# Query and key casts behind the preceding pair's first row maxima, one transfer per operand, one task per pair for PV, in a fused attention and MoE kernel on one Trainium2 core

## The chip, the cores and the metric

One core of a Trainium2 chip runs the whole program. The metric is the device time in microseconds (us), median of the runs shown.

## The reference

Three stages follow each other, all in float32. Attention has 4 batches, 8 heads, 576 rows and 64 columns per head; a routed mixture of 8 experts (top 1, 512 to 1024 to 512) and a three-way maximum layer (512 to 768 to 512) follow on the 2304 tokens.

```python
scores = scale * np.matmul(q, k.transpose(0, 1, 3, 2))
cum = np.cumsum(np.log(np.clip(f, 0.0001, 1.0)), axis=-1)
scores = np.where(causal, -1e9, scores + cum[:, :, :, None] - cum[:, :, None, :])
attn = np.exp(scores - scores.max(-1, keepdims=True))
attn = attn / (attn.sum(-1, keepdims=True) + 1e-09)
x = np.matmul(attn, v)                       # B, H, S, D -> B*S, H*D
...
expert_idx = np.argmax(logits, axis=1)       # logits = normed x @ normed emb.T / tau
out[mask] = gate_w[mask, None] * (np.maximum(x[mask] @ w1[e], 0.0) @ w2[e])
...
h = np.maximum(np.maximum(x @ w1, x @ w2), x @ w3)
return h @ w_out
```

## The kernel before, in words

Attention works on 16 pairs of heads (p = 0 to 15, four pairs to a batch). A float32 product is made of rounded high parts and remainders: for each pair, `At` holds q rounded in its rows 0 to 63 and the remainder of q in rows 64 to 127, `R1` holds k rounded (both halves), `R2` the remainder of k in rows 0 to 63 and the decay (`chi`, `clo`) in rows 64 and 65, and `Bt` a copy of rounded q with two rows of ones. A score tile is one matmul of At with R1 and one of Bt with R2 (L355 for block 0 of both heads, L360 for the others). The work that makes these operands, per pair, is in `split_tasks` (L313): loads of q and k by SP (`load_pair`), the two rounding casts `q_hi` and `k_hi` on ACT or DVE (L462 on DVE, L464 on ACT), the two remainders `k_lo` (L334) and `q_lo` (L331) on POOL, and the copy to Bt by a DMA (`q_copy`). Each operand exists three times, so pair p writes over that of pair p - 3. For pair 0 it is written out ahead of the plan (`first_split`, L274 to 281).

Blocks of rows are taken in the order 4, 0, 3, 1, 2. For each, DVE subtracts the mask and takes the row maxima (L383, L377 for block 0), ACT takes the exponential (L408), PE transposes (L421 to L429), and DVE or ACT copies into `PT` (L462, L464). `pair_out` then makes reciprocals (L473 to L476), the product with V in two groups of columns (`pv`, L488, tiles po_0 and po_1), copies them (`ot`), transposes them back with the expert embedding appended (`back`, L507, tiles pb_0 and pb_1), normalises (`norm`, L516) and stores. After the last pair of a batch a routing chain follows on DVE (L604 to L618 and further operations).

What stands on which engine, and in which order, is decided while the program is built, by a planner (`Sched`, L128): each task has an engine (or two to choose from), a cost, a priority and the tasks that it depends on; the planner takes the task that can start first, and of those that can start together the one of lowest priority number. A task with `get` needs a buffer of a pool: three score tiles `s`, eight probability tiles `P`, two `t`, two `o`, two `ot`. The order on each engine is then fixed; on the chip every instruction waits for its operands. The setup of the routing constants, among it `tri8` (L579), runs as a chain in the same plan.

```python
load = sd.task("SP", 3.3, lambda e: load_pair(p), u - 8, ready[p - 2], lat=2.0)
qh = sd.task(("ACT", "DVE"), (1.02, 0.67), q_hi, u, old + [load])
kh = sd.task(("ACT", "DVE"), (1.1, 0.8), k_hi, u, old + [load, qh])
kl = sd.task("Pool", 2.6, k_lo, u, [kh])
ql = sd.task("Pool", 2.6, q_lo, u, [qh, kl])
```

Of the kernel before, what the change touches and what calls it, by code (L numbers as in the profile page):

```python
# [6 lines left out]
F32 = mybir.dt.float32  # L7
# [122 lines left out]
class Sched:  # L130
# [8 lines left out]
        self.bias = {"DVE": 0.15, "Pool": 2.0}  # L139

    def task(self, eng, cost, fn, prio, deps=(), get=None, rel=(), lat=0.0):
        t = Task(eng if isinstance(eng, tuple) else (eng,), cost, fn, prio, get, rel, lat)
        t.deps = [d for d in deps if d is not None]
        for d in t.deps:
            if d.end is None:
                d.after.append(t)
                t.wait += 1
        if not t.wait:
            self.open.append(t)
        return t  # L150
# [27 lines left out]
    def when(self, t, eng):  # L178
        r = self.clk.get(eng, self.t0)
        for d in t.deps:  # L180
            r = max(r, d.end + (self.HOP if d.by != eng else 0.0))
        if t.get:
            pool, _ = t.get
            held = self.taken[pool]
            n = len(held) - self.bufs[pool]
            if n >= 0:
                if (pool, held[n]) not in self.freed:
                    return None
                r = max(r, self.freed[pool, held[n]] + self.HOP)
        return r  # L190

    def run(self):
        while self.open:
            best = None
            for t in self.open:
                pick = None
                for i, eng in enumerate(t.eng):
                    r = self.when(t, eng)
                    if r is None:
                        break  # L200
                    c = t.cost[i] if isinstance(t.cost, tuple) else t.cost
                    k = r + c + self.bias.get(eng, 0.0)
                    if pick is None or k < pick[0]:
                        pick = k, r, eng, c
                if pick and (best is None or (pick[1], t.prio) < best[0]):
                    best = (pick[1], t.prio), t, pick[2], pick[3]
            (r, _), t, eng, c = best
            self.open.remove(t)
            self.clk[eng] = r + c
            self.now, self.later = t, []  # L210
            t.by = eng
            t.end = r + c + t.lat
            if t.get:
                self.taken[t.get[0]].append(t.get[1])
            t.fn(eng)
            for k in t.rel:
                self.freed[k] = r + c
            for add, spec, deps in self.later:
                add(spec, deps)
            self.done(t, r + c + t.lat, eng)  # L220


def attention(tc, g, qT, kT, v, x_dram, es):
# [30 lines left out]
    def load_pair(p):  # L254
        q2 = ld.tile([128, 2, S], F32, tag="q2", name=f"q2_{p}")
        k2 = ld.tile([128, 2, S], F32, tag="k2", name=f"k2_{p}")
        for t, src in ((q2, qT), (k2, kT)):
            for r in range(2):
                nc.sync.dma_start(out=t[64 * r:64 * r + 64], in_=src[p])
        raws[p] = q2, k2  # L260

    def load_v(b):
# [51 lines left out]
    def split_tasks(p):  # L314
        i, u = p % NQ, 10 * p - 6
        load = None
        if p > 1:
            old = [fs[h, t, k] for h in (2 * p - 6, 2 * p - 5) for t in range(NBLK) for k in range(1 + (t == 4))] if p >= NQ else []
            load = sd.task("SP", 3.3, lambda e: load_pair(p), u - 8, ready[p - 2], lat=2.0)
            dec = sd.task("SP", 1.3, lambda e: load_decay(p), u - 4, old, lat=2.0)  # L320
        else:
            old, dec = [], None

        def q_hi(e):
            evict(e, At[i], raws[p][0])

        def k_hi(e):
            evict(e, R1[i], raws[p][1])

        def q_lo(e):  # L330
            nc.gpsimd.tensor_tensor(out=At[i][64:128], in0=raws[p][0][64:128], in1=At[i][64:128].bitcast(F32), op=ALU.subtract)  # L331

        def k_lo(e):
            nc.gpsimd.tensor_tensor(out=R2[i][0:64], in0=raws[p][1][0:64], in1=R1[i][0:64].bitcast(F32), op=ALU.subtract)  # L334

        def q_copy(e):
            nc.sync.dma_start(out=Bt[i][0:64].bitcast(F32), in_=At[i][0:64].bitcast(F32))

        qh = sd.task(("ACT", "DVE"), (1.02, 0.67), q_hi, u, old + [load])
        qc = sd.task("SP", 0.9, q_copy, u, [qh], lat=2.0)  # L340
        kh = sd.task(("ACT", "DVE"), (1.1, 0.8), k_hi, u, old + [load, qh])
        kl = sd.task("Pool", 2.6, k_lo, u, [kh])
        ql = sd.task("Pool", 2.6, q_lo, u, [qh, kl])
        ready[p] = [x for x in (qh, ql, qc, kh, kl, dec) if x is not None]
# [45 lines left out]
    def head(h):  # L390
# [3 lines left out]
        for t in order:  # L394
# [14 lines left out]
                                     accum_out=sums[b][0:n, t, h % H:h % H + 1])  # L409

            fe[h, t] = sd.task("ACT", 0.28 + ext / 1200, exp, slot[h, t], [fr[h, t]])
        old = [fo[p - 2, u] for u in range(2)] if p >= 2 else []
        low = [slice(64 * x, 64 * x + 64) for x in range(2)]
        for t in order:
            i0 = ROW0[t]
# [44 lines left out]
    def evict(e, out, in_):  # L460
        if e == "DVE":
            nc.vector.tensor_copy(out, in_)  # L462
        else:
            nc.scalar.activation(out=out, in_=in_, func=AF.Copy)  # L464

    def pair_out(p):
# [9 lines left out]
            nc.vector.reciprocal(rs[0], rs[0])  # L476

        rt = sd.task("DVE", 0.35, recip, u0, [fe[h, t] for h in hs for t in order])
        for u, (c0, w) in enumerate(RNG):
            na = 3 if u == 0 else 5  # L480
            o = {}

            def pv(e, u=u, c0=c0, w=w, na=na, o=o):
                po = o[0] = ps_o.tile([128, 512], F32, tag="o", name=f"po_{p}_{u}")
                for a in range(na):
                    lo = max(128 * a, c0)
                    for r in range(2):
                        nc.tensor.matmul(po[64 * r:64 * r + 64, lo - c0:w],  # L488
                                         vt[b][:, a, (2 * hp + r) * D:(2 * hp + r + 1) * D],
                                         PT[(2 * p + r) % NPT][:, a, lo:c0 + w], start=(a == 0), stop=(a == na - 1))  # L490

            ts = order
            cost = sum((c0 + w - max(128 * a, c0)) * 4 / 2400 + 0.05 for a in range(na))
            fo[p, u] = sd.task("PE", cost, pv, u0 + 1, [fv[h, t] for h in hs for t in ts] + [vdep[b]], get=("o", ("po", p, u)))

            def cp_(e, u=u, w=w, o=o):
                o[1] = op.tile([128, 320], F32, tag="ot", name=f"ot_{p}_{u}")
                evict(e, o[1][:, 0:w], o[0][:, 0:w])

            fc = sd.task(("ACT", "DVE"), (act(w), dve(w)), cp_, u0 + 2 * u - 4, [fo[p, u]], get=("ot", (p, u)), rel=[("o", ("po", p, u))])  # L500
            m = len(BLKS[u])

            def back(e, u=u, c0=c0, m=m, o=o):
                pb = o[2] = ps_o.tile([128, 512], F32, tag="o", name=f"pb_{p}_{u}")
                for j, t in enumerate(BLKS[u]):
                    i0 = ROW0[t] - c0
                    nc.tensor.matmul(pb[:, 144 * j:144 * j + 144], o[1][:, i0:i0 + 128],  # L507
                                     g.w144[:, hp].rearrange("p r c -> p (r c)"), start=True, stop=True)

            fb = sd.task("PE", 0.24 * m, back, u0 + 2 * u + 1, [fc, consts_done], get=("o", ("pb", p, u)), rel=[("ot", (p, u))])  # L510

            def norm(e, u=u, m=m, o=o):
                if hp == 0 and u == 0:
                    XL[b] = xl.tile([128, NBLK, H, DW], F32, tag="XL", name=f"XL{b}")
                t0 = BLKS[u][0]
                nc.vector.tensor_tensor(  # L516
                    out=XL[b][:, t0:t0 + m, 2 * hp:2 * hp + 2, :], in0=o[2][:, 0:144 * m].rearrange("p (s r c) -> p s r c", s=m, r=2),
                    in1=rs[0][:, t0:t0 + m].unsqueeze(3).to_broadcast([128, m, 2, DW]), op=ALU.mult)

            fn_[p, u] = sd.task("DVE", 0.07 + 0.15 * m, norm, u0 + 2 * u - 4, [fb, rt], rel=[("o", ("pb", p, u))])  # L520
# [17 lines left out]
    split_tasks(1)  # L538
    for p in range(NP):
        b, hp = divmod(p, NPAIR)  # L540
        if p + 2 < NP:
            split_tasks(p + 2) if p + 2 > 1 else None
        if hp == 1 and b + 1 < B:
            vdep[b + 1] = sd.task("SP", 3.3, lambda e, b=b: load_v(b + 1), 40 * b + 20, [fo[NPAIR * b - 1, u] for u in range(2)] if b else [], lat=2.0)
        head(2 * p)
        head(2 * p + 1)
        pair_out(p)
        if hp == NPAIR - 1:
            batch_out(b)
# [940 lines left out]
```

## Time and profile before

| what | before |
|---|---|
| time, median of 3 runs | 766.96 us (765.95 to 769.46) |
| the profiled execution | 767.35 us, span of the trace 765.5 us |
| mean granted clock of TensorE | 0.98 of full speed |
| PE busy, in matmul | 723.9 us, 95% of the span |
| DVE, ACT, POOL busy | 59%, 49%, 18% |
| q and k in DRAM | 32 transfers each of 288 KB, 64 partitions |
| PE's last matmul of attention ends at about | 210 us |

The profiled execution is one run; its span leaves out 1.85 us around the trace. PE is the engine that is busy nearly all the time; the other engines matter where PE waits for them. Granted clock is the share of TensorE's full clock that was granted over a stretch.

### The profile page before, as it was taken

The numbers are of one execution on the slowest core, as the hardware profiler recorded it, in microseconds if no ns is written. First come the engines' busy times: TensorE is split into PE (matmuls) and PEld (weight loads), VectorE is DVE, ScalarE is ACT, GpSimd is POOL, SyncE is SP. The second block draws the span as 40 slices with busy tenths as digits, with TensorE's granted clock in tenths as the row PEclk, the third lists the DMA queues.
The fourth block names the chain that finished last, engine by engine and source line by source line (L and its number), as shares of the span: only waits on it lengthen the run. The fifth ranks groups of instructions, "written<-read, shape, count | busy, mean of one in ns | idle before, by whom it ended". The sixth has DMA issues, their size and how long they took to land. (4 is left out here: it accounts for less than half of the span.)

```text
span 765.5 us, 13139 instructions
## 1 busy us (share of the span) xinstructions
PE 723.9 (95%) x4814; PEld 679.8 (89%) x4814; DVE 449.1 (59%) x1101; ACT 376.8 (49%) x871; POOL 138.9 (18%) x124
## 2 busy tenths in 40 slices
PE   1899999899949999999999999999999999999996
PEld 1688888788839999999999999989999899998994
DVE  6878888787576986888787759722212123122220
ACT  5588899699637655555565645421211212112111
POOL 7555373532030201202101000010010100101001
PEclk9999999899959999999999999999999999999999
DMA  9778886751155656647566443110000100100001
GB/s 224 201 171 188 220 199 177 167 126 33 33 176 193 223 196 203 203 148 250 190 212 244 169 166 91 49 42 0 15 29 1 42 1 0 42 1 28 15 0 44
DMA packets 44612, 90.17 MB, mean 118 GB/s; under 512 B 23320, under 2 KB 23320, under 8 KB 44544
## 3 DMA queue, kind: packets, MB, share of 16 engines
q1 hardware_dynamic: 40416, 77.70, 35.3%
q0 software_dynamic: 3152, 9.88, 3.6%
q10 hardware_dynamic: 976, 1.70, 0.6%
q8 instruction: 40, 0.66, 0.4%
q14 instruction: 28, 0.23, 0.1%
HBM read 74.97 MB, written 9.44 MB: 110 GB/s over the span
## 5 line engine op out<-in xcount | busy, mean ns | idle before, releaser
L1267 DVE TENSOR_TENSOR tm<-pm,tm 128x384 f32<-128x384 f32 x72 | 40.1, 557 | 178.8 <-PE pm L937 178.6
L937 PE MATMUL pm<-x_y,m 128*128 128x384 f32 x432 | 144.4, 334 | 0.0
L935 PE MATMUL pm<-x_y,m 128*128 128x384 f32 x432 | 144.4, 334 | 0.0
L936 PE MATMUL pm<-x_y,m 128*128 128x384 f32 x432 | 144.4, 334 | 0.0
L981 DVE TENSOR_TENSOR w<-stg,w 128x1024 fp32r<-128x1024 f32 x64 | 77.9, 1223 | 26.1 <-ACT w L964 25.8
L408 ACT ACTIVATE P<-P,nm 128x576 f32<-128x576 f32 (+2 forms) x144 | 84.0, 585 | 12.3 <-DVE nm L383 12.0
L964 ACT ACTIVATE w<-stg 128x1024 fp32r<-128x1024 f32 x62 | 65.3, 1056 | 37.7 <-issue 12.3
L936 PEld LDWEIGHTS pm<-x_y,m 128*128 128x128 f32 x432 | 81.1, 188 | 0.3
L935 PEld LDWEIGHTS pm<-x_y,m 128*128 128x128 f32 x432 | 81.1, 188 | 0.2
L937 PEld LDWEIGHTS pm<-x_y,m 128*128 128x128 f32 x432 | 81.1, 188 | 0.0
L935 PE MATMUL ph<-x,w 128*128 128x384 f32 (+7 forms) x256 | 79.7, 311 | 0.7 <-ACT x L964 0.7
L935 PE MATMUL py<-h,w 128*128 128x384 f32 (+7 forms) x256 | 79.6, 311 | 0.0
L936 PE MATMUL ph<-x,w 128*128 128x384 f32 (+7 forms) x256 | 79.2, 309 | 0.4 <-issue 0.4
L937 PE MATMUL ph<-x,w 128*128 128x384 f32 (+7 forms) x256 | 78.8, 308 | 0.0
L1302 POOL DMA_INDIRECT out_dram<-oo,ctidx x18 | 17.7, 986 | 334.1 <-ACT oo L1299 331.0
L937 PE MATMUL py<-h,w 128*128 128x384 f32 (+7 forms) x256 | 78.2, 306 | 0.0
L936 PE MATMUL py<-h,w 128*128 128x384 f32 (+7 forms) x256 | 78.2, 306 | 0.0
L360 PE MATMUL s<-R,At 128*128 128x288 f32 (+3 forms) x160 | 61.2, 388 | 17.3 <-DVE At L279 10.6
L964 ACT ACTIVATE g<-tm 128x384 fp32r<-128x384 f32 x36 | 18.8, 524 | 111.0 <-DVE tm L1267 111.0
L1091 POOL DMA_INDIRECT gat<-x_dram,gidx x23 | 26.8, 1165 | 205.3 <-PE xt L1098 158.1
L383 DVE CUSTOM_DVE_ANT_0 P<-s,mask 128x288 f32<-128x288 f32 (+3 forms) x128 | 58.3, 477 | 5.7 <-PE s L360 3.7
L425 PE MATMUL t<-ident,P 128*128 128x128 f32 x320 | 58.7, 283 | 0.3 <-ACT PT L464 0.3
(254 smaller groups left out, 1552.4 us busy)
## 6 DMA issues: line engine op xcount, KB each, us to landing
stg<-in_w_dram SPq DMA_DIRECT2D x61, 512.0 KB
q<-in_q_dram SPq DMA_DIRECT2D x32, 288.0 KB
k<-in_k_dram SPq DMA_DIRECT2D x32, 288.0 KB
sd<-in_m_dram SPq DMA_DIRECT2D x18, 512.0 KB
Bt<-At SPq DMA_DIRECT2D x16, 288.0 KB
V<-in_v_dram SPq DMA_DIRECT2D x4, 1024.0 KB
x_dram<-XL SPq DMA_DIRECT2D x62, 64.0 KB
sd_o<-in_mo_dram SPq DMA_DIRECT2D x6, 512.0 KB
```

The lines of the kernel that those rows point to most:

```text
L360: nc.tensor.matmul(st[:, 0:wp], lt[0:kk, r, q0:q0 + 128], rt[0:kk, r, j0:j0 + wp], start=(ps_i == 0), stop=(ps_i == 1))
L383: nc.vector.tensor_tensor_reduce(out=P[0:n, j0:j0 + w], in0=st_.pop((h, t, k))[0:n, 0:w], in1=g.mask[0:n, m0:m0 + w], scale=-0.125, scalar ...
L408: nc.scalar.activation(out=P[0:n, 0:ext], in_=P[0:n, 0:ext], func=AF.Exp, bias=nm[0:n, k:k + 1], scale=-1.0, accum_out=sums[b][0:n, t, h % ...
L425: nc.tensor.transpose(w[:, 128 * a:128 * a + 128], P[:, 128 * a:128 * a + 128], g.ident)
L935: nc.tensor.matmul(out, whi, xhi, start=start, stop=False)
L936: nc.tensor.matmul(out, whi, xlo, start=False, stop=False)
L937: nc.tensor.matmul(out, wlo, xhi, start=False, stop=stop)
L964: nc.scalar.activation(out=out, in_=in_, func=AF.Copy)
L981: ENG[e].tensor_tensor(out=w[:, 1], in0=t, in1=w[:, 0].bitcast(F32), op=ALU.subtract)
L1091: nc.gpsimd.indirect_dma_start(out=t[0:n], out_offset=None, in_=x_dram, in_offset=bass.IndirectOffsetOnAxis(ap=idx, axis=0))
L1267: nc.vector.tensor_tensor(out=mx[0], in0=mx["p", w][:, 0:MC], in1=mx[0], op=ALU.max)
L1302: nc.gpsimd.indirect_dma_start(out=out, out_offset=bass.IndirectOffsetOnAxis(ap=g.sidx[:, col:col + 1], axis=0), in_=o[1], in_offset=None, ...
```

## The change

Three edits. The first gives the cast of q (and by it that of k) a further dependence: the row maxima of block 4 of the first head of the pair ahead; and the tasks of pair p + 1 are given to the planner between the two heads of pair p, where those of pair p + 2 were given ahead of pair p. The second lays q and k out twice in DRAM, along the partitions, so that one transfer of 128 partitions takes the place of two of 64, and states a lower cost and a longer latency for it. The third makes the two groups of `pv` one task that takes both `o` buffers; the planner's `get` becomes a list for that.

```diff
-            for r in range(2):
-                nc.sync.dma_start(out=t[64 * r:64 * r + 64], in_=src[p])
+            nc.sync.dma_start(out=t, in_=src[p])
...
-            load = sd.task("SP", 3.3, lambda e: load_pair(p), u - 8, ready[p - 2], lat=2.0)
+            load = sd.task("SP", 0.9, lambda e: load_pair(p), u - 8, ready[p - 2], lat=4.5)
...
-        qh = sd.task(("ACT", "DVE"), (1.02, 0.67), q_hi, u, old + [load])
+        idle = [fr[2 * p - 2, order[0]]] if p > 1 else []
+        qh = sd.task(("ACT", "DVE"), (1.02, 0.67), q_hi, u, old + [load] + idle)
...
-        for u, (c0, w) in enumerate(RNG):
-            na = 3 if u == 0 else 5
-            o = {}
-
-            def pv(e, u=u, c0=c0, w=w, na=na, o=o):
-                po = o[0] = ps_o.tile([128, 512], F32, tag="o", name=f"po_{p}_{u}")
+        po_ = {}
+
+        def pv(e):
+            for u, (c0, w) in enumerate(RNG):
+                na = 3 if u == 0 else 5
+                po = po_[u] = ps_o.tile([128, 512], F32, tag="o", name=f"po_{p}_{u}")
...
-            fo[p, u] = sd.task("PE", cost, pv, u0 + 1, [fv[h, t] for h in hs for t in ts] + [vdep[b]], get=("o", ("po", p, u)))
+        fo[p] = sd.task("PE", 3.05, pv, u0 + 1, [fv[h, t] for h in hs for t in order] + [vdep[b]],
+                        get=[("o", ("po", p, u)) for u in range(2)])
...
-        if p + 2 < NP:
-            split_tasks(p + 2) if p + 2 > 1 else None
...
         head(2 * p)
+        if 1 < p + 1 < NP:
+            split_tasks(p + 1)
         head(2 * p + 1)
...
-    qp = _np.stack([_np.roll(qp[:, 0], -64, axis=1), qp[:, 1]], axis=1)
+    qp = _np.stack([_np.roll(qp[:, 0], -64, axis=1), qp[:, 1]], axis=1).transpose(0, 3, 1, 2)
+    kp = a["k"].reshape(B * NPAIR, 2, S, D).transpose(0, 3, 1, 2)
-        "q": c(qp.transpose(0, 3, 1, 2)),
-        "k": c(a["k"].reshape(B * NPAIR, 2, S, D).transpose(0, 3, 1, 2)),
+        "q": _np.concatenate([qp, qp], axis=1),
+        "k": _np.concatenate([kp, kp], axis=1),
```

Lines below L313 move down by one to three: L462 is L464 after, L579 is L582, L604 to L618 are L607 to L621.

The order moves most on DVE. The first place is pair 2, whose casts are the first that the planner places anew. Before (P_4, P_0, P_3 and P_1 are row maxima by block; the `nm` rows that read each out are left out, as are copies):

```order
L462 CAST At_115<-q_2_206 128x1152
L462 CAST R_121<-k_2_207 128x1152
L383 ISA P_4_371,nm_4_372<-s_4_0_346,mask 128x288
L383 ISA P_4_371,nm_4_372<-s_4_1_349,mask,nm_4_372 128x288
L377 ISA P_0_388,nm_0_389<-s_0_0_353,mask_86 128x128
L383 ISA P_3_411,nm_3_412<-s_3_0_385,mask 128x448
L579 TENSOR_TENSOR tri_419<-ioe,iok 128x64
L582 MEMSET caps 128x1 x8
L584 MEMSET ones 128x128
```

After:

```order
L385 ISA P_4_352,nm_4_353<-s_4_0_341,mask 128x288
L385 ISA P_4_352,nm_4_353<-s_4_1_348,mask,nm_4_353 128x288
L379 ISA P_0_382,nm_0_383<-s_0_0_355,mask_86 128x128
L464 CAST At_115<-q_2_202 128x1152
L385 ISA P_3_397,nm_3_398<-s_3_0_379,mask 128x448
L582 TENSOR_TENSOR tri_406<-ioe,iok 128x64
L585 MEMSET caps 128x1 x8
L385 ISA P_1_438,nm_1_439<-s_1_0_387,mask 128x192
L464 CAST R_121<-k_2_203 128x1152
```

The two casts, which stood next to each other ahead of the maxima of block 4, now stand behind both maxima of block 4 and that of block 0, with three maxima or setup operations between the two; tri8 has come between them.

The second place is the routing chain of batch 1 (L604 to L618 before, L607 to L621 after; XL is what `norm` writes, pb_1 the second tile of `back`). Before:

```order
L383 ISA P_4_1919,nm_4_1920<-s_4_0_1908,mask 128x288
L383 ISA P_4_1919,nm_4_1920<-s_4_1_1915,mask,nm_4_1920 128x288
L516 TENSOR_TENSOR XL_1363<-pb_1_1929,rs_1660 128x2x144
L604 TENSOR_REDUCE L<-XL_1363 128x40
L607 TENSOR_REDUCE lmax<-L 128x5
L610 TENSOR_TENSOR e_1956<-L,lmax 128x40
L612 TENSOR_TENSOR e_1956<-e_1956,w_337 128x40
L615 TENSOR_REDUCE e_1974<-e_1956 128x5
L618 SCALAR_TENSOR_TENSOR oh<-e_1956,e_1974 128x40
L383 ISA P_3_1981,nm_3_1982<-s_3_0_1935,mask 128x448
```

After:

```order
L464 CAST At_114<-q_10_1635 128x1152
L385 ISA P_3_1851,nm_3_1852<-s_3_0_1835,mask 128x448
L385 ISA P_1_1859,nm_1_1860<-s_1_0_1840,mask 128x192
L464 CAST R_120<-k_10_1636 128x1152
L519 TENSOR_TENSOR XL_1299<-pb_1_1855,rs_1644 128x2x144
L607 TENSOR_REDUCE L<-XL_1299 128x40
L610 TENSOR_REDUCE lmax<-L 128x5
L613 TENSOR_TENSOR e_1900<-L,lmax 128x40
L615 TENSOR_TENSOR e_1900<-e_1900,w_333 128x40
L618 TENSOR_REDUCE e_1922<-e_1900 128x5
L621 SCALAR_TENSOR_TENSOR oh<-e_1900,e_1922 128x40
L385 ISA P_2_1927,nm_2_1928<-s_2_0_1848,mask 128x320
```

Here the chain now follows the cast of k_10 on DVE, behind which POOL has the two remainders of pair 10; before, no cast stood ahead of it. The chain of batch 0 stands in the same way behind the cast of k_6; that of batch 2 stands behind the cast of k_14 and three maxima.

## Rows read from the trace of the kernel before

**Rows 1.** Stretches: width; busy of PE, PEld, DVE, ACT, POOL; granted clock; DMA share; GB/s.
```profile
30.00:40.00 10.00, 7.88 (x48) 5.65 (x48) 7.18 (x36) 6.12 (x21) 3.75 (x2) 0.83 0.52 129
140.00:160.00 20.00, 17.10 (x121) 14.25 (x121) 15.05 (x45) 13.72 (x46) 9.26 (x4) 0.83 0.51 114
```

**Rows 2.** The same view while q and k load, and while a V load runs.
```profile
6.00:9.00 3.00, 0.00 (x0) 0.00 (x0) 0.68 (x1) 1.16 (x1) 1.28 (x1) 1.00 1.04 224
25.00:27.00 2.00, 2.00 (x9) 1.48 (x8) 1.65 (x10) 1.06 (x4) 0.00 (x0) 1.00 1.04 371
```

**Rows 3.** Timeline of the start: start, duration, engine, line, names [idle before <-releaser].
```profile
7.72 1.40 POOL L279 TENSOR_TENSOR At<-q,At 64x576 fp32r<-64x576 f32 x1 [2.79 <-ACT At L275]
9.03 0.76 DVE L277 CAST R<-k 128x1152 fp32r<-128x1152 f32 x1 [2.35 <-DMA k<-in_k_dram]
15.55 0.58 PE L360 MATMUL s<-R,Bt 66*128 66x288 f32 x1 [4.31 <-DMA R<-clo]
16.17 0.46 DVE L383 CUSTOM_DVE_ANT_0 P<-s,mask 128x288 f32<-128x288 f32 x1 [1.38 <-PE s L360]
```

**Rows 4.** Timeline at 31 us, POOL, DVE and PE.
```profile
31.21 2.62 POOL L331 TENSOR_TENSOR At<-q,At 64x1152 fp32r<-64x1152 f32 x1
31.77 2.14 DVE L579 TENSOR_TENSOR tri<-ioe,iok 128x64 f32<-128x64 f32 x1
34.51 0.40 PE L360 MATMUL s<-R,At 128*128 128x288 f32 x1 [2.06 <-DVE nm L383]
```

**Rows 5.** Timeline from 138 to 146 us, POOL, DVE and PE.
```profile
138.34 2.65 POOL L334 TENSOR_TENSOR R<-k,R 64x1152 fp32r<-64x1152 f32 x1 [11.71 <-PE s L360]
139.35 2.26 DVE L462 CAST At<-q 128x1152 fp32r<-128x1152 f32 x1
141.06 3.02 POOL L331 TENSOR_TENSOR At<-q,At 64x1152 fp32r<-64x1152 f32 x1
141.53 3.17 DVE L462 CAST R<-k 128x1152 fp32r<-128x1152 f32 x1
145.13 0.74 PE L360 MATMUL s<-R,At 128*128 128x448 f32 x1 [2.90 <-DVE nm L383]
```

**Rows 6.** Timeline: one period, a row maximum, and a k cast with its low half.
```profile
46.32 0.30 PE L360 MATMUL s<-R,Bt 66*128 66x288 f32 x1
47.00 0.52 DVE L383 CUSTOM_DVE_ANT_0 P<-s,mask,nm 128x288 f32<-128x288 f32 x1
156.93 0.34 PE L355 MATMUL s<-R,At 128*128 128x192 f32 x1
160.35 0.71 DVE L462 CAST R<-k 128x1152 fp32r<-128x1152 f32 x1
161.29 2.64 POOL L334 TENSOR_TENSOR R<-k,R 64x1152 fp32r<-64x1152 f32 x1 [11.03 <-DVE R L462]
167.77 0.34 PE L355 MATMUL s<-R,At 128*128 128x192 f32 x1
```

**Rows 7.** Costliest groups: row maxima of all widths (busy, mean ns | idle before).
```profile
L383 DVE CUSTOM_DVE_ANT_0 P<-s,mask 128x288 f32<-128x288 f32 (+3 forms) x128 | 58.3, 477 | 5.7 <-PE s L360 3.7
```

**Rows 8.** Timeline from 80 to 84 us: routing of batch 0 beside POOL.
```profile
80.66 2.66 POOL L331 TENSOR_TENSOR At<-q,At 64x1152 fp32r<-64x1152 f32 x1
81.46 0.77 DVE L604 TENSOR_REDUCE L<-XL 128x40 f32<-128x320 f32 x1
82.49 0.88 DVE L610 TENSOR_TENSOR e<-L,lmax 128x40 f32<-128x40 f32 x1
83.41 0.20 DVE L612 TENSOR_TENSOR e<-e,w 128x40 f32<-128x40 f32 x1
```

**Rows 9.** Groups of DVE by shape from 20 to 200 us: normalisation of two blocks.
```profile
L516 DVE TENSOR_TENSOR XL<-pb,rs 128x288 f32<-128x288 f32 x14 | 6.4, 456 | 0.4
```

**Rows 10.** Timeline of PE at the end of attention.
```profile
205.47 0.66 PE L507 MATMUL pb<-w,ot 128*128 128x144 f32 x4
206.06 2.94 PE L488 MATMUL po<-PT,V 128*64 128x320 f32 x32
```

More of the change, by code (lines that the diff above doesn't have):

```diff
@@ L141, in task @@
     def task(self, eng, cost, fn, prio, deps=(), get=None, rel=(), lat=0.0):
+        get = get if isinstance(get, list) else [get] if get else []
         t = Task(eng if isinstance(eng, tuple) else (eng,), cost, fn, prio, get, rel, lat)
@@ L181, in when @@
             r = max(r, d.end + (self.HOP if d.by != eng else 0.0))
-        if t.get:
-            pool, _ = t.get
+        more = {}
+        for pool, _ in t.get:
             held = self.taken[pool]
-            n = len(held) - self.bufs[pool]
+            n = len(held) + more.get(pool, 0) - self.bufs[pool]
+            more[pool] = more.get(pool, 0) + 1
             if n >= 0:
-                if (pool, held[n]) not in self.freed:
+                if n >= len(held) or (pool, held[n]) not in self.freed:
                     return None
@@ L212, in run @@
             t.end = r + c + t.lat
-            if t.get:
-                self.taken[t.get[0]].append(t.get[1])
+            for pool, key in t.get:
+                self.taken[pool].append(key)
             t.fn(eng)
@@ L411, in head @@
             fe[h, t] = sd.task("ACT", 0.28 + ext / 1200, exp, slot[h, t], [fr[h, t]])
-        old = [fo[p - 2, u] for u in range(2)] if p >= 2 else []
+        old = [fo[p - 2]] if p >= 2 else []
         low = [slice(64 * x, 64 * x + 64) for x in range(2)]
@@ L490, in pv @@
                                          PT[(2 * p + r) % NPT][:, a, lo:c0 + w], start=(a == 0), stop=(a == na - 1))
-            ts = order
-            cost = sum((c0 + w - max(128 * a, c0)) * 4 / 2400 + 0.05 for a in range(na))
-            fo[p, u] = sd.task("PE", cost, pv, u0 + 1, [fv[h, t] for h in hs for t in ts] + [vdep[b]], get=("o", ("po", p, u)))
+        fo[p] = sd.task("PE", 3.05, pv, u0 + 1, [fv[h, t] for h in hs for t in order] + [vdep[b]],
+                        get=[("o", ("po", p, u)) for u in range(2)])
+        for u, (c0, w) in enumerate(RNG):
+            o = {}
             def cp_(e, u=u, w=w, o=o):
                 o[1] = op.tile([128, 320], F32, tag="ot", name=f"ot_{p}_{u}")
-                evict(e, o[1][:, 0:w], o[0][:, 0:w])
-            fc = sd.task(("ACT", "DVE"), (act(w), dve(w)), cp_, u0 + 2 * u - 4, [fo[p, u]], get=("ot", (p, u)), rel=[("o", ("po", p, u))])
+                evict(e, o[1][:, 0:w], po_[u][:, 0:w])
+            fc = sd.task(("ACT", "DVE"), (act(w), dve(w)), cp_, u0 + 2 * u - 4, [fo[p]], get=("ot", (p, u)), rel=[("o", ("po", p, u))])
             m = len(BLKS[u])
@@ L540, in attention @@
         b, hp = divmod(p, NPAIR)
-        if p + 2 < NP:
-            split_tasks(p + 2) if p + 2 > 1 else None
         if hp == 1 and b + 1 < B:
-            vdep[b + 1] = sd.task("SP", 3.3, lambda e, b=b: load_v(b + 1), 40 * b + 20, [fo[NPAIR * b - 1, u] for u in range(2)] if b else [], lat=2.0)
+            vdep[b + 1] = sd.task("SP", 3.3, lambda e, b=b: load_v(b + 1), 40 * b + 20, [fo[NPAIR * b - 1]] if b else [], lat=2.0)
         head(2 * p)
+        if 1 < p + 1 < NP:
+            split_tasks(p + 1)
         head(2 * p + 1)
```

## Prediction, made before the run

> **What bounds the kernel now.** The page comes first: PE is busy 95% of the span, and in its 40 slices PE falls below 9 tenths only within the first 230 us and at the very end. The change touches attention alone, some 210 us, so what it can win or lose is PE's idle time there, and TensorE's clock. The windows show both at once [rows 1]: from 30 to 40 us PE worked 7.88 of 10 us and the granted clock was 0.83; from 140 to 160 us it worked 17.10 of 20, again at 0.83. [...]
>
> The timeline then tells what PE waited for. At 34.51 it waited 2.06 us for a row maximum; DVE was late because tri8, an operation on 64 elements, took 2.14 us beside a POOL operation of 2.62 us [rows 4]. At 145.13 it waited 2.90 us for another; there the cast of q took 2.26 us and that of k 3.17, where 0.71 is a cast's time when POOL is idle [rows 5, 6]. The ends tell the mechanism: the first cast ended at 141.61, 0.62 behind the end of POOL's operation (140.99), the second at 144.70, 0.62 behind the end of the next one (144.08). So DVE stood still until POOL's whole operation was done, then did its work. Last the start [rows 3]: PE waits 4.31 us for `clo`, which lies in SP's queue behind the loads of q and k.
>
> **Start: gain 2.5 us.** The tiles of q and k of pairs 0 and 1 are eight transfers of 288 KB, 2.36 MB. In 64 partitions they ran at 224 GB/s with the DMA engines' share at 1.04; a load of V over 128 partitions ran at 371 with the same share [rows 2]. That is 10.5 us before and 6.4 after: `clo`, behind all of it, lands 4.1 earlier, and k of pair 0, behind half of it, 2.1. What is late next is DVE: the k cast (9.03) starts when POOL's half of the q remainder (7.72 + 1.40) ends, and that half comes some 1.1 earlier with q. With the 1.38 us that DVE stood idle ahead of the first maximum [rows 3], that is 1.1 + 1.38 = 2.5. Bounds: nothing, and 4.1. That the loads cost SP fewer issues counts nothing: SP is not waited for after the start.
>
> **tri8: gain 3.8 us.** In the new order tri8 stands between the casts of pair 2, when POOL has nothing to do: the k remainder waits for the k cast, the q remainder for that. So PE's 2.06 and the clock's 1.7 go.
>
> **Casts that meet POOL: gain 6.3 us.** Around 139 us q and k of two pairs followed each other, and casts of one pair met remainders of the other. Now a pair's casts come one pair at a time and its remainders end before the next pair's casts. The wait of 2.90 and the clock's 3.4 go. Gains: 2.5 + 3.8 + 6.3 = 12.6.
>
> **Shorter lead: loss 3.2 us.** The remainder of q must be there when the pair's first score matmul comes. It now counts from the second score matmul of block 4 of the preceding first head: 1.20 to the end of its maximum (46.32 to 47.52), then two maxima at 0.48 each [rows 7], a q cast of 0.71, one more maximum of 0.48, 0.94 from the start of the k cast to POOL's start, 2.72 from POOL's first start to its second (138.34 to 141.06), and 2.64 for the second [rows 5, 6]: 9.7 us. PE's work in between is one period, 10.84 (156.93 to 167.77), less what now stands ahead of that matmul, counted in the new order for each pair: 9.1 to 11.7, and less than 9.7 by 0.5 to 0.6 for pairs 4, 8 and 13; pair 2 is short by 0.6 (tri8 and the memsets come between) and pair 15 by 0.9 (a routing and two norms do). The sum is 3.2; pairs 6 and 10, short by less, fall into the next term. Bounds: nothing, if DVE's work overlaps more than I count, and the case of the longer lag below.
>
> **Routing of batches 0 and 1: loss 9.0 us.** Both chains now stand right behind a k cast, the place where POOL begins two operations in a row. Let that cast start at 0. POOL then works from 0.94 to 3.58 and from 3.66 to 6.3 [rows 5, 6]. DVE comes to the comparison (L610, L613 after) at 0.71 + 0.46 (norm) + 0.77 + 0.20 = 2.14 [rows 6, 8, 9]. In the trace of before it stood still for just such an operation: it took 0.88 and ended at 83.37, when POOL's had ended at 83.32 [rows 8]. So it waits until 3.6 (1.44 us), and the multiplication behind it (L612, L615 after) comes when POOL's second operation has begun and waits to 6.3 (some 2.5 us). The next row maximum ends at about 7.3. PE has work until about 4.5: the product with V, 2.94 [rows 10], and 1.6 of transposes, back and ready score tiles; then three score tiles are full. Its wait is 2.8 each time, and the clock behind each takes 1.7, the smaller of the two rows [rows 1]: 2 x 4.5 = 9.0. Bounds for each: nothing, and 2.8 + 3.4 = 6.2.
>
> What the rows don't show is a second wait of the same chain: in before the multiplication took 0.20, since POOL was through [rows 8]. By that row alone only the first wait is certain, which PE's 4.5 us hide; this term is then nothing.
>
> [...]
>
> **Tail: loss 0.6 us.** One `back` of pair 14 (0.66 with what it shares) stood between the last transposes and the last product with V [rows 10]; it now comes earlier, and PE waits there for the copies instead. Bounds 0 and 0.7. The product as one task of 2.94 costs nothing else: both `o` buffers are free by then, since the norms ahead are done, and it frees what it did before.
>
> **Sum.** -12.6 + 3.2 + 9.0 + 0.6 = +0.2 us. The profiled execution took 767.35, so the changed kernel would take 767.55 in its place. That execution stands 0.39 above the median of the runs, 766.96, so the forecast is 767.2. Own range of this case: the terms are off by 2 to 3 each in either sense, 763 to 772.
>
> **Rivals.**
> - *Faster: the routing waits cost PE nothing* (only the first of them is met, or PE has more work in hand than I count). 767.2 - 9.0 = 758.2, own range 755 to 761. For: the hole of batch 0 in before [rows 8] has no wait of PE behind it. Against: two casts in a row each stood through one operation of POOL [rows 5].
> - *Slower: the lag grows.* The 1.20 us from the score matmul to the end of its maximum is a row where DVE was free; where copies or norms are ahead in DVE's queue it is more. At 2.0, 0.8 longer, each of the five short pairs loses 0.75 more and three further ones (3, 9, 12, with 9.9 us of work) about 0.45: 5 us, 772.2. It decides from a lag of about 1.5 on. For: DVE was busy 15.05 of 20 us [rows 1], and casts now stand among its maxima. Against: PE that waits also lets DVE catch up.
> - *The change doesn't do what it says:* one transfer per operand runs no faster than two did, since the 1.04 shows all DMA engines busy already. Then the 2.5 of the start are gone: 769.7.
>
> **How the numbers follow.** The forecast has 0.44, the faster rival 0.29, the slower 0.18, the slow transfer 0.09. About 0.5% (3.8 us) is what a measurement here tells from no change: below 763.1 or above 770.8. The forecast's own spread puts about a sixth of it on each side, 0.07. Faster: 0.28 + 0.07 = 0.35. Slower: 0.16 + 0.07 + 0.02 = 0.25. Within: 0.40. The range 755 to 774 takes in the faster rival's own range and the slower with 2 us on top; it leaves about 0.1 on either side together with what I haven't thought of.
>
> **What would show it.** q and k of the start at about 370 GB/s and the first maximum at 13.7 us; tri8 at about 0.2 us; no q or k cast on DVE above 0.8 us; comparison and multiplication of batches 0 and 1 at about 1.6 and 2.7 us, PE waiting some 3 us for a maximum right behind, with a granted clock below 1; waits of 0.5 to 0.9 us for the q remainder at the first score matmuls of pairs 2, 4, 8, 13 and 15. The forecast is wrong if PE does not wait behind the routing, or if it waits at every pair's start.

## The result, and the profile after

The changed kernel takes 771.41 us (median of 9 runs, 769.21 to 772.44), the kernel before 766.96 in its 9 runs beside it; the ratio is 1.0054, with a 95% interval of 1.0037 to 1.0070. That is about 4 us slower, just over the 0.5% named in the prediction, inside the range of 755 to 774 and 4 above the forecast of 767.2. The profiled execution took 771.86 us. In the trace, PE's last matmul of attention ends at 215.96 us, where it ended at 210.41 before; 1 of the 5.5 us is won back in the stages behind.

The page's head for the changed kernel (span; busy time of each engine and its share):

```profile
span 770.1 us, 13079 instructions
...
PE 727.7 (95%) x4814; PEld 682.3 (89%) x4814; DVE 455.7 (59%) x1115; ACT 372.8 (48%) x857; POOL 136.4 (18%) x124
```

PE is as busy as before, 95%. The windows of the changed kernel (columns as in [rows 1]):

```profile
4.00:7.00 3.00, 0.00 (x0) 0.00 (x0) 2.87 (x4) 1.19 (x2) 1.42 (x3) 1.00 1.02 421
30.00:40.00 10.00, 9.91 (x85) 8.31 (x85) 8.34 (x48) 7.95 (x26) 5.29 (x2) 1.00 0.37 102
80.00:100.00 20.00, 19.01 (x141) 17.00 (x142) 15.30 (x63) 15.83 (x47) 5.29 (x2) 0.83 0.35 97
120.00:140.00 20.00, 16.54 (x125) 14.34 (x124) 16.18 (x47) 14.43 (x48) 5.26 (x2) 0.83 0.61 202
180.00:200.00 20.00, 18.18 (x159) 16.06 (x155) 15.66 (x58) 15.35 (x49) 6.52 (x3) 0.91 0.19 39
```

The first of them answers to [rows 2]: 421 GB/s while q and k load, where 224 went before. From 30 to 40 us PE now works 9.91 us at full clock [rows 1]. The three others are new: twice 0.83 and once 0.91, where before the only such stretch of attention after 40 us was the one from 140 to 160. What lies there is the routing of batches 0, 1 and 2. The timeline of the first, DVE, POOL and PE:

```profile
73.30 0.75 DVE L464 CAST R<-k 128x1152 fp32r<-128x1152 f32 x1
...
74.28 2.64 POOL L335 TENSOR_TENSOR R<-k,R 64x1152 fp32r<-64x1152 f32 x1 [6.10 <-DVE R L464]
...
74.86 0.76 DVE L607 TENSOR_REDUCE L<-XL 128x40 f32<-128x320 f32 x1
...
75.89 1.09 DVE L613 TENSOR_TENSOR e<-L,lmax 128x40 f32<-128x40 f32 x1
...
77.00 2.61 POOL L332 TENSOR_TENSOR At<-q,At 64x1152 fp32r<-64x1152 f32 x1
77.02 2.65 DVE L615 TENSOR_TENSOR e<-e,w 128x40 f32<-128x40 f32 x1
...
80.57 0.36 PE L362 MATMUL s<-R,At 128*128 128x192 f32 x1 [1.98 <-DVE nm L385]
```

This is the mechanism of the prediction, line by line. The k cast starts at 73.30, POOL's two remainders follow from 74.28 and 77.00. The reduction L607 runs through the first at 0.76. The comparison L613 takes 1.09 us and ends as that remainder ends (76.92); the multiplication L615 takes 2.65 and ends as the second one does (79.61). PE waits 1.98 us for the row maximum behind them. Batch 1, same view:

```profile
126.06 1.52 DVE L613 TENSOR_TENSOR e<-L,lmax 128x40 f32<-128x40 f32 x1
...
127.60 2.62 POOL L332 TENSOR_TENSOR At<-q,At 64x1152 fp32r<-64x1152 f32 x1
127.62 2.66 DVE L615 TENSOR_TENSOR e<-e,w 128x40 f32<-128x40 f32 x1
...
131.21 0.47 PE L362 MATMUL s<-R,At 128*128 128x448 f32 x1 [2.20 <-DVE nm L385]
...
133.48 0.19 PE L627 MATMUL pr<-oh,tris 128*128 128x40 f16 x1 [1.05 <-ACT ot L466]
```

L613 and L615 take 1.52 and 2.66, PE waits 2.20; then it waits again, 1.05 us, with `pr`, the matmul of the routing that counts ranks. That one needs an `o` buffer, and with the product with V as one task both are taken until an `ot` copy has run. Batch 2:

```profile
178.59 2.64 POOL L332 TENSOR_TENSOR At<-q,At 64x1152 fp32r<-64x1152 f32 x1
...
179.03 2.25 DVE L613 TENSOR_TENSOR e<-L,lmax 128x40 f32<-128x40 f32 x1
...
185.21 0.18 PE L627 MATMUL pr<-oh,tris 128*128 128x40 f16 x1 [1.76 <-DVE ot L464]
```

Here only the comparison met a remainder, 2.25 us, and `pr` cost 1.76.

The start, in the same view:

```profile
13.57 0.46 DVE L385 CUSTOM_DVE_ANT_0 P<-s,mask 128x288 f32<-128x288 f32 x1
...
16.22 4.59 DVE L112 COPY w<-ident 64x256 f32<-64x256 f32 x2
...
18.05 2.61 POOL L332 TENSOR_TENSOR At<-q,At 64x1152 fp32r<-64x1152 f32 x1
...
21.40 0.74 PE L362 MATMUL s<-R,At 128*128 128x448 f32 x1 [2.42 <-DVE nm L385]
```

The first row maximum begins at 13.57, against 16.17 [rows 3]. Since all is earlier, though, both copies of the identity into w144 (L112) now fall beside POOL's remainders of pair 1 and take 4.59 us together, where they took 1.90 and 0.30 before; PE waits 2.42 for the maximum behind them. Last the two places that the change was to clear, tri8 in the timeline and the casts of pairs on DVE as groups by shape from 10 to 212 us (count, total, mean ns):

```profile
29.95 0.22 DVE L582 TENSOR_TENSOR tri<-ioe,iok 128x64 f32<-128x64 f32 x1
```

```profile
L464 DVE CAST R<-k 128x1152 fp32r<-128x1152 f32 x14 | 10.5, 751 | 0.0
L464 DVE CAST At<-q 128x1152 fp32r<-128x1152 f32 x12 | 9.1, 755 | 0.0
```

tri8 takes 0.22 us where it took 2.14 [rows 4], and none of these casts meets POOL any more; with the same counts the totals were 14.0 and 11.5 us before.

### The profile page after: what moved, and what is told of

Same layout as the page of the kernel before. It is cut to its first block, busy times and chain, and to the rows that moved or that the text cites. A ratio compares the mean times of both kernels' runs of the same rounds, so it can differ in the third digit from the quotient of the medians.

```text
span 770.1 us, 13079 instructions
## 1 busy us (share of the span) xinstructions
PE 727.7 (95%) x4814; PEld 682.3 (89%) x4814; DVE 455.7 (59%) x1115; ACT 372.8 (48%) x857; POOL 136.4 (18%) x124
## 5 line engine op out<-in xcount | busy, mean ns | idle before, releaser
L466 ACT ACTIVATE PT<-t 128x384 f32<-128x384 f32 (+4 forms) x129 | 50.6, 404 | 22.5 <-PE t L427 16.6
```

## The experiments

All are edits of the changed kernel but one. The last column is the ratio to the kernel before, run beside it. That kernel's own median was 766.8 to 766.9 us beside the experiments and 764.7 beside the last four rows, so these four are compared with the others by their ratios.

| kernel | median us | ratio (95%) |
|---|---|---|
| changed kernel | 771.41 | 1.0054 (1.0037 to 1.0070) |
| second edit undone | 773.00 | 1.0081 (1.0049 to 1.0114) |
| first edit undone | 777.51 | 1.0129 (1.0067 to 1.0191) |
| third edit undone | 780.72 | 1.0185 (1.0129 to 1.0241) |
| routing behind POOL | 761.36 | 0.9944 (0.9917 to 0.9972) |
| routing behind POOL, third edit undone | 762.47 | 0.9959 (0.9930 to 0.9988) |
| routing and w144 behind POOL | 758.64 | 0.9894 (0.9847 to 0.9942) |
| remainders in quarters | 759.49 | 0.9899 (0.9867 to 0.9931) |
| routing and w144 behind POOL, quarters | 758.14 | 0.9879 (0.9831 to 0.9927) |
| kernel before, quarters | 758.83 | 0.9922 (0.9892 to 0.9953) |
| first edit undone, quarters | 756.32 | 0.9876 (0.9828 to 0.9924) |
| second edit undone, quarters | 761.66 | 0.9952 (0.9929 to 0.9974) |
| third edit undone, quarters | 768.85 | 1.0055 (1.0030 to 1.0080) |

### The routing planned behind POOL's remainders

```diff
-        if hp == NPAIR - 1:
-            batch_out(b)
+        if hp == 1 and b:
+            batch_out(b - 1, ready[p + 1][1])
+    batch_out(B - 1, None)
...
-    def batch_out(b):
+    def batch_out(b, low):
...
-        last[0] = sd.chain(g.batch_done(b, lambda: XL[b][:, :, :, D:DW]), pr, deps + [last[0], consts_done])
+        last[0] = sd.chain(g.batch_done(b, lambda: XL[b][:, :, :, D:DW]), pr, deps + [last[0], consts_done, low])
```

> The changed kernel, all three edits in, with one more dependence: the routing chain of batches 0 to 2 is planned behind POOL's remainder of q of pairs 6, 10 and 14. Theory (DVE stands still behind POOL): comparison and multiplication take 0.2 us each, 758 to 763. Rival one (lead): no change, 771. Rival two (the one task for PV holds both o buffers): the waits of the rank matmul stay, some 3 us, and only part is won, 765 to 768.

Measured: 761.36, 10 us below the changed kernel. The timeline at the routing of batch 0 (L614 and L616 are comparison and multiplication here) and the window over it:

```profile
77.17 2.64 POOL L332 TENSOR_TENSOR At<-q,At 64x1152 fp32r<-64x1152 f32 x1
...
80.14 0.75 DVE L608 TENSOR_REDUCE L<-XL 128x40 f32<-128x320 f32 x1
...
81.16 0.20 DVE L614 TENSOR_TENSOR e<-L,lmax 128x40 f32<-128x40 f32 x1
...
81.40 0.20 DVE L616 TENSOR_TENSOR e<-e,w 128x40 f32<-128x40 f32 x1
```

```profile
80.00:100.00 20.00, 18.39 (x153) 15.29 (x154) 17.89 (x69) 15.17 (x48) 5.40 (x3) 1.00 0.55 163
```

Both take 0.20 us once POOL is through, and the clock stays at 1.00. The three waits of `pr` are gone too. So the place of the routing is worth 10 us, and rival one (the lead) has no part in it. Not all of it is POOL's: the edit also removes the waits of `pr`, and these stay in part when POOL's instructions are short (the run with the remainders in quarters, below).

### Each edit undone alone

The third edit:

```diff
-        fo[p] = sd.task("PE", 3.05, pv, u0 + 1, [fv[h, t] for h in hs for t in order] + [vdep[b]],
-                        get=[("o", ("po", p, u)) for u in range(2)])
+            fo[p, u] = sd.task("PE", cost, pv, u0 + 1, [fv[h, t] for h in hs for t in ts] + [vdep[b]], get=("o", ("po", p, u)))
```

> The changed kernel with its third edit alone undone: the product with V is two tasks again. In the order that comes out, the routing chains of batches 0 to 2 stand between the cast of q and that of k of pairs 6, 10 and 14, where POOL has nothing to do, and no longer behind the cast of k. Theory (DVE stands still behind POOL's two remainders in the routing): comparison and multiplication take 0.2 us each, the three waits of PE behind them (1.98, 2.20 and 1.76 us) and the lower clock there are gone, some 9 to 13 us, so 758 to 763. Rival one (the lead is too short): the cast of k now comes some 2 us later in those three pairs, so 771 or more, with PE waiting for the remainder of q there. Rival two (the one task holds both o buffers and the rank matmul of the routing waits for one): only its three waits of 0.39, 1.05 and 1.76 go, 768.

Measured: 780.72, 9 us above the changed kernel; the expectation missed. Comparison and multiplication do take 0.2 us, ahead of the k cast as planned, but now the later operations of the chain stand behind it. The timeline at batch 0 (L747 and L648 are `rm` and `rc` of the routing):

```profile
78.03 2.63 POOL L335 TENSOR_TENSOR R<-k,R 64x1152 fp32r<-64x1152 f32 x1 [7.63 <-DVE r L637]
78.17 2.52 DVE L747 TENSOR_SCALAR rm<-rank 128x5 int32<-128x5 int32 x1
...
80.74 3.28 POOL L332 TENSOR_TENSOR At<-q,At 64x1152 fp32r<-64x1152 f32 x1
81.47 2.58 DVE L648 TENSOR_TENSOR rc<-ioc,rq 128x15 f32<-128x15 f32 x1
...
85.04 0.74 PE L362 MATMUL s<-R,At 128*128 128x448 f32 x1 [4.37 <-DVE nm L385]
```

`rm`, five values per partition, takes 2.52 us, `rc` 2.58, and PE waits 4.37; batches 1 and 2 repeat it with 4.34 and 4.35. The theory of the collision holds, but I had followed only two operations of a chain of some fifteen.

The first edit:

```diff
-        qh = sd.task(("ACT", "DVE"), (1.02, 0.67), q_hi, u, old + [load] + idle)
+        qh = sd.task(("ACT", "DVE"), (1.02, 0.67), q_hi, u, old + [load])
...
+        if p + 2 < NP:
+            split_tasks(p + 2) if p + 2 > 1 else None
...
-        if 1 < p + 1 < NP:
-            split_tasks(p + 1)
```

> The changed kernel with its first edit alone undone: casts depend on the loads and on the operand buffers only, and the pair after next is given to the planner ahead of a pair, as before. Theory: casts meet remainders of another pair again (casts of 2 to 3 us, tri8 near 2 us), the start stays earlier by 1 to 2 us; where the routing chains now fall decides, 763 to 769. Rival one (lead): with the old lead of 6 to 16 us back, the time is below that of the kernel before, 762 to 764, with no wait of PE at a pair's first score matmul.

Measured: 777.51, 8 above the upper end of what was expected. Remainders lie 6 us and more ahead of their matmuls again; what that is worth by itself this run can't tell, since collisions come back with it: tri8 takes 2.31 us again, casts meet remainders at three places, and the routing does at two. The timeline at one place of each (L463 is the cast, L648 again `rc`):

```profile
113.37 3.03 POOL L332 TENSOR_TENSOR At<-q,At 64x1152 fp32r<-64x1152 f32 x1
...
113.84 3.18 DVE L463 CAST R<-k 128x1152 fp32r<-128x1152 f32 x1
...
118.16 0.36 PE L361 MATMUL s<-R,At 128*128 128x192 f32 x1 [2.48 <-DVE nm L384]
...
144.31 2.58 DVE L648 TENSOR_TENSOR rc<-ioc,rq 128x15 f32<-128x15 f32 x1
...
148.00 0.29 PE L724 MATMUL ptab<-rr,ohp 128*128 128x24 f16 x5 [4.15 <-DVE XL L518]
```

The second edit:

```diff
-            nc.sync.dma_start(out=t, in_=src[p])
+            for r in range(2):
+                nc.sync.dma_start(out=t[64 * r:64 * r + 64], in_=src[p, 64 * r:64 * r + 64])
```

> The changed kernel with its second edit alone undone: two transfers of 64 partitions for q and for k, at the planner's old cost. The order on PE and DVE stays that of the changed kernel. Theory: only the start changes; the first score matmul comes about 1.2 us later and the first maximum 2 to 3 us later, of which the copy of w144 that meets POOL at 18 us gives back part; 772 to 774. Rival (a load per pair that is faster or slower matters all along attention): 776 or more, or 769 or less.

Measured: 773.00, as expected, with the same three places of the routing; the intervals overlap, so the 1.6 us are not told from nothing here. In the profiled executions pair 1 begins 1.3 us later than in the changed kernel (28.66 against 27.32).

### The remainders in quarters

```diff
-            nc.gpsimd.tensor_tensor(out=At[i][64:128], in0=raws[p][0][64:128], in1=At[i][64:128].bitcast(F32), op=ALU.subtract)
+            for r in range(2):
+                for c in (slice(0, 288), slice(288, 576)):
+                    nc.gpsimd.tensor_tensor(out=At[i][64:128, r, c], in0=raws[p][0][64:128, r, c], in1=At[i][64:128, r, c].bitcast(F32), op=ALU.subtract)
```

`k_lo` is cut in the same way. This leaves the order on DVE and PE as it is in the changed kernel and alters only how long one POOL instruction lasts.

> The changed kernel with each POOL remainder (2.6 us) cut in four instructions of a quarter of the columns each; the order on PE and DVE stays that of the changed kernel, the routing chains still stand behind the casts of k_6, k_10 and k_14. Theory (DVE stands still until the one POOL instruction that it met is through, and no longer): comparison and multiplication take at most some 0.7 to 0.9 us each instead of 1.09 to 2.66, the waits of PE behind them (1.98, 2.20, 1.76 us) shrink below 1 us and the clock there stays nearer 1; 762 to 767. Rival one (the chain is late because of what it does or where it stands, POOL's instruction is not what holds it): no change, 771. Rival two (an instruction has a price of its own on POOL): the remainders end later than the 0.2 to 1.4 us that they have in hand, PE waits for them at every pair, 773 or more.

Measured: 759.49, 12 us below the changed kernel and below the 762 to 767 expected. Timeline at batch 0 (L617 and L619 are comparison and multiplication):

```profile
72.13 3.07 POOL L339 TENSOR_TENSOR R<-k,R 64x288 fp32r<-64x288 f32 x4 [5.21 <-DVE R L468]
...
73.74 0.76 DVE L617 TENSOR_TENSOR e<-L,lmax 128x40 f32<-128x40 f32 x1
...
74.54 0.72 DVE L619 TENSOR_TENSOR e<-e,w 128x40 f32<-128x40 f32 x1
...
78.99 0.18 PE L631 MATMUL pr<-oh,tris 128*128 128x40 f16 x1 [0.97 <-ACT ot L470]
```

The multiplication took 0.72 us where it took 2.65, with POOL busy all the while: DVE waits for one instruction, not for the pair of remainders. A remainder in four takes 3.07 us instead of 2.64, and no pair waits for it. The stretch over this routing, from the block 0 matmul of pair 5 to that of pair 8, in the changed kernel and here (columns as in [rows 1]):

```profile
70.12:109.86 39.74, 37.25 (x298) 32.05 (x296) 33.19 (x116) 30.30 (x94) 15.83 (x6) 0.91 0.55 161
67.97:103.54 35.57, 34.35 (x297) 29.34 (x296) 31.26 (x116) 29.98 (x94) 18.44 (x24) 1.00 0.64 184
```

It is 4.2 us shorter. In the same way pair 8 to pair 12, over the routing of batch 1, is 5.2 shorter, and pair 12 to pair 15, over that of batch 2, 1.6. What stays are the waits of `pr` for an `o` buffer, 0.97, 0.60 and 1.25 us: long POOL instructions are not what they need.

> The kernel before, none of the three edits, with POOL's remainders in quarters and nothing else. Theory (of the change's effect only the places where DVE meets POOL count, besides the start): the waits of 2.06 us at 34 us and 2.90 us at 145 us shrink below 1 us and the clock behind them comes back, 759 to 762, within 3 us of the changed kernel with quarters (759.5). Rival (the edits are worth time in themselves, and the collisions hid it): 764 or more. Rival (they cost in themselves): 757 or less.

Measured: 758.83, just under the range that was expected. Beside the changed kernel with quarters, ratios of 0.9922 and 0.9899 with intervals that overlap widely: with POOL's instructions short, change or no change makes no difference that can be told. The 0.5% of the change are where long POOL instructions fall. The stretch from pair 11 to pair 12, where the casts met POOL, in the kernel before and here:

```profile
141.23:156.93 15.70, 12.80 (x85) 10.67 (x83) 10.86 (x33) 9.61 (x32) 8.11 (x3) 0.78 0.50 113
136.90:147.77 10.87, 10.13 (x85) 8.75 (x83) 8.62 (x32) 9.62 (x32) 10.31 (x13) 1.00 0.64 145
```

The same 85 matmuls take 4.8 us less. At the end of attention, whole remainders cost the kernel before 9.1 us (210.41 against 201.32 here) and the changed kernel 13.1 (215.96 against 202.82 with quarters): it cleared 9 us of collisions and made 13.

> The changed kernel with remainders in quarters and its first edit undone (casts early, as before). Theory (the short lead costs nothing, and the early casts nothing either once POOL's instructions are short): 758 to 762. Rival (the lead): 757 or less, since the remainders have 6 us and more in hand. Undoing this edit cost 6 us with whole remainders.

Measured: 756.32, below the range that was expected and on the rival's side of 757; but the ratio is 0.9876 beside 0.9899, with intervals that overlap widely. A cost of the short lead is not told from nothing, and the early casts cost nothing that shows.

> The changed kernel with remainders in quarters and its second edit undone (two transfers of 64 partitions). Theory: only the start, some 1.3 us of the first score matmul and 3 to 4 us of the first maximum, less what the copy of w144 gives back; 761 to 763. Rival (nothing, hidden): 759 to 760.

Measured: 761.66, as expected, ratio 0.9952 beside 0.9899, with intervals that only just touch. In the profiled executions pair 1 begins 2.0 us later than with the edit (27.30 against 25.32) and pair 15 still 2.0 (188.20 against 186.21): the second edit is worth 2 us there, all of it at the start.

> The changed kernel with remainders in quarters and its third edit undone (product with V as two tasks). Theory: without long POOL instructions the order that it gives is as good; the waits of the rank matmul for an o buffer (0.97, 0.60 and 1.25 us) go, 757 to 759. Rival (the order itself was bad, not the collisions): it stays 5 us or more above the changed kernel with quarters, 765 or more, as it was 9 us above without.

Measured: 768.85, above the changed kernel with quarters by 9 us in the medians and by 12 in the ratios; the theory missed, and the rival is nearer. The timeline at batch 0 and the window over it:

```profile
76.20 3.63 POOL L339 TENSOR_TENSOR R<-k,R 64x288 fp32r<-64x288 f32 x4 [6.86 <-DVE r L641]
76.34 0.68 DVE L751 TENSOR_SCALAR rm<-rank 128x5 int32<-128x5 int32 x1
...
77.06 1.38 DVE L759 TENSOR_TENSOR ohp<-iota,rm 128x640 f16<-128x640 f32 x1
...
78.36 0.76 DVE L652 TENSOR_TENSOR rc<-ioc,rq 128x15 f32<-128x15 f32 x1
...
80.64 0.47 PE L366 MATMUL s<-R,At 128*128 128x448 f32 x1 [1.77 <-DVE nm L389]
```

```profile
80.00:100.00 20.00, 19.25 (x144) 16.58 (x144) 16.82 (x65) 15.96 (x53) 9.26 (x12) 0.91 0.46 146
```

Four operations of the chain stand in a row behind the k cast (`rm`, `ohp`, `rc` and one more), each held by a quarter, some 2.2 us together; PE waits 1.77, and 1.74 at each of the other two batches, each time with the clock at 0.91. In the changed kernel with quarters the clock stays at 1.00 from 40 to 200 us. Three times 20 x 0.09, my estimate of what the lower clock took, is 5.4 us, and the waits are 1.7 us more in sum than there: 7.1 of the 8.9 us by which attention ends later (211.72 against 202.82). Another 1.3 us by the profiled executions lie in the stages behind; their cause stays open. As the quarters still hold four operations, the runs don't show what this order would cost without any hold.

### Versions with fewer collisions

> The kernel with the routing planned behind POOL's remainders, and the third edit undone (product with V as two tasks). In the changed kernel undoing it cost 9 us, with later operations of the routing meeting POOL. Theory (the third edit moves collisions and is worth nothing itself): no operation of DVE meets POOL here either, 760 to 763, as with the one task. Rival (the one task itself is worth time, since PE goes through 32 matmuls without a break): 765 or more. Rival (it costs, since it holds both o buffers): 759 or less.

Measured: 762.47, as with the one task, though not free of collisions: the chain's last operation (L655), 0.17 us in the changed kernel, took 2.61 beside a remainder of 2.62 at batch 0, with a wait of PE of 1.33 behind it. Where the routing is out of POOL's way, the third edit makes no difference that these runs can tell; in the other orders it moves the chain.

For the next, the step of the setup that copies into w144 gets a dependence:

```diff
-    yield dict(eng="DVE", cost=0.4)
+    yield dict(eng="DVE", cost=0.4, more=g.low_1)
...
+    g.low_1 = lambda: [ready[1][1]]
```

> The kernel with the routing planned behind POOL's remainders, and the copies of the identity into w144 planned behind POOL's remainder of q of pair 1 (in the changed kernel they took 4.6 us beside it, and PE waited 2.42 us at 21 us). Theory: that wait goes, 758 to 760; tri8 now stands near POOL's remainders of pair 2 and may take 2 us again, which would give the gain back, 761.

Measured: 758.64. The wait at 21 us is gone, and from 15 to 36 us PE waits at no place longer than 0.31 us.

> All three together: routing and w144 planned behind POOL, remainders in quarters. Theory: whatever still meets POOL waits at most some 0.7 us, 756 to 760. Rival (quarters end later and the short lead has nothing in hand): 763 or more, with PE waiting for the remainder of q at the first score matmul of pairs.

Measured: 758.14. Five of the versions, from 756.3 to 759.5, beat both kernels, the kernel before by 0.8 to 1.2%; these runs don't tell them apart. The one with the fewest edits is the kernel before with its remainders in quarters.

## Why the prediction was near, and which steps failed

The time was inside the range, and the bound case that I thought likeliest, no change, was missed by little: the sum named the right mechanism, had several sizes wrong and left two losses out. That it came so near is in part luck, as the sum at the end shows. Times of a pair are read at its block 0 matmul (L355, L357 after).

- **Start** (forecast 2.5 gained). The first maximum came at 13.57, 2.6 earlier. At block 0 of pair 1 only 1.7 were left (29.00 to 27.32): the L112 copies had met POOL. With quarters in both kernels the gain at that place is 2.65 (27.97 to 25.32). The step that failed is "what is late next is DVE": I followed it to the first maximum and not on.
- **tri8** (3.8). From pair 1 to pair 2 PE needed 13.86 us before and 10.71 for the same 85 matmuls in the kernel before with quarters: 3.1. The changed kernel took 10.78. Right, a little too large.
- **Casts that meet POOL** (6.3). They are gone, but not with 6.3. Short POOL instructions took 4.8 off that stretch in the kernel before and left a wait of 0.74. The clock's 1.7 and 3.4 in the sum are estimates, the width of a stretch of [rows 1] times what its granted clock lacks of 1 (10 x 0.17, 20 x 0.17); no run shows work lost to the clock by itself. In the trace of before the clock stands at 0.50 from 36 to 38 us and from 146 to 150, behind the two waits, and what came off with them, wait and clock together, was 3.1 at tri8 and 4.8 here. So a wait plus all of that estimate counts somewhat too much: 2.16 us of wait and 3.4 of clock make 5.6, and 4.8 came. At the routing of batch 0 it does so as well: quarters took off 1.4 of wait (1.98 + 0.39 - 0.97) and, by the same estimate, 3.4 of clock, 4.8, and 4.2 came.
- **Shorter lead** (3.2 lost). It cost nothing. The timeline of pair 13, one of those that the sum made short:

```profile
168.69 2.64 POOL L332 TENSOR_TENSOR At<-q,At 64x1152 fp32r<-64x1152 f32 x1
...
171.57 0.38 PE L362 MATMUL s<-R,At 128*128 128x288 f32 x1
```

The remainder is through at 171.33, 0.24 us ahead of the matmul. In the other pairs from 2 on it is 0.3 to 1.5, more where PE waited for something else, and never too late. For this pair I had both sides wrong: from the score matmul at 162.05, from which I counted, to the end of the remainder it took 9.28 us and not 9.7, and PE had 9.52 us of work to the matmul at 171.57 and not 9.1 to 9.2. The slower rival rested on this step and falls with it.
- **Routing** (9.0 lost, at batches 0 and 1). It came as described: 1.09 and 2.65, 1.52 and 2.66 against 1.6 and 2.7, waits of 1.98 and 2.20 against 2.8, a clock lower than the one that I took, 0.83 over 20 us. No row of before shows the multiplication waiting, the second wait that the 9.0 needs; that step was my estimate, with the two casts of [rows 5] as its nearest like. The runs showed it: 2.65 and 2.66 us beside remainders of 2.61 and 2.62, and 0.20 with POOL through. Batch 2 I had left out as standing three maxima behind its cast. By the prediction's own figures, a remainder runs from 3.66 to 6.3 us behind the cast; its comparison came at 4.15 (cast at 174.88, L613 at 179.03). By the quarters the three cost 4.2, 5.2 and 1.6 where the sum had 4.5, 4.5 and nothing: 11.0 instead of 9.0.
- **The product as one task** (nothing). "Both o buffers are free by then" looked at what the task needs and not at who comes next: `pr` waited 0.39, 1.05 and 1.76 us for a buffer, twice for a copy on ACT and once for one on DVE. With quarters it waited 0.97, 0.60 and 1.25, so 2.8 us of waits are there without long POOL instructions too; with two tasks in place of one (third edit undone, whole or in quarters) it waited less than 0.3 us at these places.
- **Tail** (0.6 lost). From the last product with V to the last back matmul PE took 4.35 us before (206.06 to 210.41) and 4.78 after (211.18 to 215.96): 0.4.

The sum from what was measured: -1.7 - 3.1 - 4.8 + 11.0 + 2.8 + 0.4 = 4.6, beside 4.4 between the medians and 5.5 at the end of attention; about 1 us of the latter stays open. The sum of the prediction had +0.2. Its loss of 3.2 for the lead did not come, while 4.4 that it did not have did, batch 2 and the waits of `pr`. That the one covered most of the other is luck: without the 3.2 the forecast would have stood at 764.0 and missed by 7. The faster rival needed the routing waits to be hidden, and they were not; the transfers do what the change says.

## What to carry to other kernels

Before an order is judged by which engine is free, list the short operations of one engine that can be held by a long instruction of another (here 0.20 us became 2.65), and follow every one of them through the new order, not the two that look worst; a cleared collision here came back at a place with less work behind it. Shortening the long instruction was one small edit, and it won 0.8% on the kernel before, where the three edits lost 0.5%. It doesn't make the order indifferent: with the third edit undone the kernel stayed slow.

## What the runs showed of the hardware that I had not expected

- One input is enough to be held: `rm`, a TENSOR_SCALAR on five values, took 2.52 us beside POOL and `rq`, its like, 0.16 behind it; the L112 copies took 4.59 for two.
- POOL is held as well: in the run with the third edit undone the remainder of 80.74 took 3.28 us instead of 2.64, behind `ohp` of 0.82 us, which had begun at 80.73.
- The 128-partition transfers ran at 421 GB/s, above the 371 of the V load that I had gone by.
